# Batch 1's query and even-key sums and batch 2's query sums on GpSimd, noise terms behind the last copy of an expert, zero stores at earlier steps

## The chip, the cores and the metric

The kernel runs on one core of one Trainium2 chip. Its time is the device time of one execution in microseconds (us); lower is better. Engines are named as in the profile: PE is TensorE (PEld its weight loads), DVE is VectorE, ACT is ScalarE, POOL is GpSimd, SP is SyncE, which here only issues transfers.

## The reference

Three stages in a row on 2304 tokens of width 512 (4 batches of 576, 8 heads of 64):

```
q_d, k_d, v_d = means of 4 consecutive positions of q, k, v        # 144 of 576
out_up    = repeat(softmax(scale * q_d k_d^T) v_d, 4)              # pooled attention
out_local = softmax(scale * q k^T  where |i - j| < 4) v            # window attention
x = out_up + out_local                                             # tokens x 512

# first mixture of experts: 8 experts, top 1, only tokens with x @ w_skip > 0
x[do_compute] += gate * relu(x w1[e]) w2[e]

# second: 8 experts, top 2 of  x w_gate + log1p(exp(x w_noise)) * noise
out = sum over the two experts of  weight * relu(x u1[e]) u2[e]
```

## The kernel before

**Attention.** The tokens are cut into 18 tiles of 128. Work on them is a hand-written pipeline of units: `Local(t)` is the window attention of tile t, `Pooled(b, u)` one of five units (u = 4, 0, 1, 2, 3) of the pooled attention of batch b. `push` puts one unit into the pipeline (a slot): its scores on PE, the maximum and subtraction (`soft`) on DVE, then whatever is due in this slot, the exponential on ACT, and the products with the values of the unit three slots earlier, whose results DVE reads out of one of two PSUM banks of the name pB. `schedule(n, f)` puts f into the slot n places on. The instructions of PE, ACT, DVE and POOL stand in just this order in each engine's queue; the order on SP is set by a planner. The slots that matter here: tiles 0 to 2 are slots 0 to 2, tile 3 is slot 3, units (0,4), (0,0), (0,1) are slots 4 to 6, tile 4 is slot 7, (0,2) and (0,3) are 8 and 9, tile 5 is 10, (1,4), (1,0), (1,1) are 11 to 13, tile 6 is 14, (1,2) and (1,3) are 15 and 16.

`load_qk(b)` loads queries into `qT` (two buffers, 128 x 4 x 576) and keys into `kTs[b % 2]` (128 x 2 x 4 x 576: plane 0 for even, plane 1 for odd heads; SP's queue brings plane 0, ACT's plane 1). `pool_qk(b, n)` sums groups of four positions for `Pooled`: n = 0 to 7 are single `tensor_reduce` calls on DVE (line 769), queries into `qd[b]` for even n, even keys into `kd` plane 0 for odd n; four of them go into one slot, four into the next. n = 8 to 10 are odd keys: three whole additions on POOL (line 772), each over 128 x 576 with a stride of four elements on its input. In batch 0 the odd keys are summed on DVE too (line 765).

`load_wall` loads the gate weights before tile 3; three slots later DVE copies them into `wall` (line 1166), which `x_part` of tile 0 first reads in slot 17. `x_add` (line 989) adds the pooled result to a tile on POOL.

**First mixture.** Experts run one after another: `half_up` multiplies with w1 (line 558), `turn` transposes the next expert's tokens (line 537), `down(0)` and `down(1)` multiply with w2 (line 571) and each is followed by a DVE copy of its PSUM bank into `yT` (line 573). `part` of the next expert's loop multiplies `yT` by `wall` (line 579) and so waits for both copies. Into the loop are sprinkled: `clear(i)`, a store of 768 rows of zeros to `out` issued on ACT's queue (line 1668); four of them clear `out` for the second mixture's additions. At expert e = 4 (`E - LATE`): after f2 = 2, `ahead.noisy.load()` reads the logits `l2_d` back (tile `nal`), and at d2 = 0, right behind the first copy, `soft()` puts Exp and Ln of them on ACT and `choose()` the noisy scores and the choice of the second mixture's first experts on DVE (lines 1289 to 1376).

**Second mixture.** Three multiplications of each pair of halves (lines 1576 and 1593); PE works nearly without a pause.

Of the kernel before, what the change touches and what calls it, by code (L numbers as in the profile page):

```python
# [10 lines left out]
F32 = mybir.dt.float32  # L11
# [4 lines left out]
OP = mybir.AluOpType  # L16
# [37 lines left out]
TURN, PART, LOGIT = 1, 2, 3  # L54
PTAG, LTAG, LTAG0 = "pT", "pB", "pW"
LATE = 4
AHEAD = 2
SOFT = 4
LOADW = 41
# [18 lines left out]
NEP = 3  # L78
EPS = 48
ONDVE = (0,)  # L80
NVG = 1
XB = 8
UB = 4
# [18 lines left out]
def moe_attention_kernel(ctx, tc, q, k, v, w_skip, w_gate, w1, w2, g2, n2, noise, u1, u2, out, dbg=None):  # L102
# [507 lines left out]
    with ExitStack() as actx:  # L610
# [135 lines left out]
        def load_qk(b):  # L746

            held["k", b % 2] = b
            qT[b] = at.tile([128, 4, S], F32, name="qT", bufs=2)
            (nc.gpsimd if b == 1 else nc.sync).dma_start(qT[b], q[b])  # L750
            for g in range(2):
                (nc.sync, nc.scalar)[g].dma_start(kTs[b % 2][g:128:2, g], k[b, 64 * g:64 * g + 64])

        def pool_qk(b, n):


            assert held["k", b % 2] == b
            held["kd", b % 2] = (b, n)
            if n == 0:
                qd[b] = at.tile([128, 4, NPOOL], F32, name="qd", bufs=2)  # L760
            kd, kT = kds[b % 2], kTs[b % 2]
            if n >= 8 and b in ONDVE:
                for i in range(n - 8, 4, 3):
                    o, x = kd[:, i, 1], kT[:, 1, i]
                    nc.vector.tensor_reduce(o, x.rearrange("p (g r) -> p g r", r=4), axis=AX.X, op=OP.add)
            elif n < 8:
                i = n // 2
                o, x = (qd[b][:, i], qT[b][:, i]) if n % 2 == 0 else (kd[:, i, 0], kT[:, 0, i])
                nc.vector.tensor_reduce(o, x.rearrange("p (g r) -> p g r", r=4), axis=AX.X, op=OP.add)
            else:  # L770
                o, x = kd[:, :, 1], kT[:, 1].rearrange("p a (g r) -> p a g r", r=4)
                nc.gpsimd.tensor_tensor(o, x[:, :, :, 0] if n == 8 else o, x[:, :, :, n - 7], op=OP.add)
# [255 lines left out]
        def schedule(n, f, *args):  # L1028
            later.setdefault(len(pipe) + n, []).append(lambda: f(*args))
# [132 lines left out]
        def load_wall():  # L1162
            t = at.tile([128, 25, KD], F32, name="gates", bufs=1)
            for o, w in ((0, w_gate), (8, w_skip), (9, g2), (17, n2)):
                nc.gpsimd.dma_start(t[:, o:o + w.shape[1] // KD, :], w.rearrange("p (e k) -> p e k", k=KD))
            schedule(3, lambda: nc.vector.tensor_copy(wall[:, :, 0:25], t.rearrange("p e k -> p k e")))

        pooled_after = {}
        for b in range(B):
# [2 lines left out]
        for t in range(NT):  # L1172
            for b in range(B):
                if LOADQK[b] == t:
                    load_qk(b)
                if POOLQK[b] == t:
                    for n in range(8):
                        schedule(n // QKS, pool_qk, b, n)
                    for n in range(3):
                        schedule(n // 2 if b in ONDVE else n, pool_qk, b, n + 8)  # L1180
                if b == 0 and t == EXP4 and UPE:
                    schedule(0, expansion)
                if POOLV[b] == t:
                    schedule(0, pool_v, b, 0)
                    schedule(VS, pool_v, b, 1)
            if t == 3:
                load_wall()
            if t < 3:
                schedule(0, lambda: None)
                schedule(0, lambda: None)  # L1190
                schedule(0, (start_1, start_2, start_3)[t])
            push(Local(t))
            for b, u in pooled_after.get(t, []):
                push(Pooled(b, u))
# [408 lines left out]
    with ExitStack() as mctx:  # L1603
# [70 lines left out]
        for e in range(E):  # L1674
            x = ex1[e]
            x.wa, x.wb = w1_tiles[e], w2_tiles[e]
            side = []
            if e == E - 2:
                la, side = split_weights(1, 0)
                la()  # L1680
            elif e == E - 1:
                lb, side = split_weights(2, 0)
                lb()
            for f2 in range(KF // 2):
                x.half_up(2 * f2)
                if f2 == 0 and prev is not None:
                    prev.part()
                elif f2 == 3 and e == 0:
                    ahead1.part()
                x.half_up(2 * f2 + 1)  # L1690
                if dbg is not None and "b1" in dbg and f2 == 3:
                    return
                if prev is not None and f2 < len(prev.blocks):
                    prev.finish(f2)()
                if f2 == 2 and e + 3 < E:
                    ex1[e + 3].gather()
                if f2 == 2 and 1 <= e <= 4:
                    clear(6 * (e - 1))
                if e == 0 and f2 == 1:
                    rg1 = m1.tile([128, NT, 3, C1], BF, name="rg1", bufs=1)  # L1700
                    spread(rg1, ohc1, g31, NT, 3, C1)
                if e == 0 and f2 == 2:
                    p = bank("pT", [BLK1, 3, C1])
                    table(p, lhs1, rg1, NT)
                    joined(egt1, p)
                    run(by_rank(gt1, egt1, NB1, rt, "ranked"))
                if e == 0 and f2 == 3:
                    ahead1.finish(0)()
                if e == E - LATE and f2 == 2:
                    ahead.noisy.load()  # L1710
                if e == E - LATE + 1:
                    if f2 == 1:
                        ahead.pl.count()
                        run(ahead.place(0))
                    elif f2 == 2:
                        run(ahead.place(1))
                if e > E - LATE + 1:
                    run(steps, NS)
                if e == E - 1:
                    if f2 < EARLY:  # L1720
                        ex2[0].prep(f2)
                if side and f2 > 1:
                    side.pop(0)()
            if e + 1 < E:
                for b in range(len(ex1[e + 1].blocks)):
                    ex1[e + 1].turn(b)
                load_experts(e + 2, nc.scalar)
            for d2 in range(KD // 2):
                x.down(d2)
                run(side, 1)  # L1730
                if e == E - LATE + 1 and d2 == 0:
                    ahead.tokens()
                    ex2[0].gather(EARLY, ahead.gidx)
                    ex2[1].gather(5 - EARLY, ahead.gidx[:, EARLY:])
                    steps = ahead.gates()
                    run(steps, 6)
                if e == E - LATE and d2 == 0:
                    ahead.noisy.soft()
                    run(ahead.choose())
            prev = x  # L1740
# [211 lines left out]
```

## Time and profile before

| what | us |
|---|---|
| median of 3 runs | 788.83 (785.14 to 790.14) |
| the profiled execution | 785.06 |
| its span, first to last instruction | 783.2 |
| attention, until the first expert's products | about 0 to 136 |
| first mixture | about 136 to 317 |
| second mixture | about 317 to 783 |

| engine | busy us of the span | share |
|---|---|---|
| PE | 755.0 | 96% |
| DVE | 360.1 | 46% |
| ACT | 249.2 | 32% |
| POOL | 239.2 | 31% |

The page's shares are means over stages with different limits, so the argument goes by stretches: the table of windows shows who is busy where, the timelines of PE, DVE, ACT and POOL show what each did in order and what ended its idle time (in brackets: the idle time, and what released it), and the list of issues shows how long transfers took to land.

### The profile page before, as it was taken

The page shows a single profiled execution, that of the slowest core. Times are in us where ns is not written, and L with a number is a line of the kernel's source. Part 1 is how long each engine was busy: PE and PEld are TensorE (multiplying, and loading weights), DVE is VectorE, ACT ScalarE, POOL GpSimd, SP SyncE. Part 2 cuts the span into 40 slices and gives each one's busy share as a digit, 9 for nine tenths or more (in the row PEclk, how much of TensorE's full clock was granted, in tenths as well). Part 3 has the DMA queues.
Part 4 walks back from the last instruction along what each step waited for, and adds up shares of the span by engine and source line. Part 5 has one row for each costly group of instructions (what it writes and reads, how often), then busy time and mean ns, then how long its engine had stood idle before and what let it go on. Part 6 is the DMA issues. An engine that isn't in the chain of part 4 may idle for free.

```text
span 783.2 us, 15164 instructions
## 1 busy us (share of the span) xinstructions
PE 755.0 (96%) x6215; PEld 663.5 (85%) x6215; DVE 360.1 (46%) x817; ACT 249.2 (32%) x492; POOL 239.2 (31%) x248
## 2 busy tenths in 40 slices
PE   6989998999999999999999999999999999999996
PEld 3566785999999899989998898898998997997984
DVE  6997887610111665468864343353242343342200
ACT  3444553111111234224333433243233333333211
POOL 8432422211232341133374305205215115002012
PEclk9899999999999999999999999999999999999999
DMA  8888578699689883331555726426526336333013
GB/s 284 285 250 284 156 191 267 179 369 359 231 281 323 308 311 125 102 69 18 142 188 154 202 81 164 104 81 172 118 84 176 84 110 155 81 87 71 8 16 46
DMA packets 61128, 131.51 MB, mean 168 GB/s; under 512 B 15585, under 2 KB 16928, under 8 KB 59520
## 3 DMA queue, kind: packets, MB, share of 16 engines
q1 hardware_dynamic: 31552, 56.64, 23.0%
q10 hardware_dynamic: 17248, 46.66, 16.5%
q0 software_dynamic: 12256, 27.21, 16.4%
q8 instruction: 50, 0.82, 0.4%
q14 instruction: 22, 0.18, 0.1%
HBM read 101.86 MB, written 23.91 MB: 161 GB/s over the span
## 4 chain that ended last, share of the span: by engine, by line
PE 74%; DMA 2%; issue 2%; DVE 1%; ACT 1%; POOL 0%; POOLq 0%; DVEq 0%; ACTq 0%
PE pY L1593 27%; PE pH L1576 26%; PE pH L558 8%; PE pY L571 8%; PE pT L1561 2%; DMA nal<-l_d 1%; PE pT L590 1%; DMA rows<-x_d,ix2g 1%; PE pT L344 1%; PE pT L537 1%; PE pH L579 0%; POOL out L315 0%; DVE w L335 0%; DMA l_d<-x,ix1w 0%; PE pH L595 0%
## 5 line engine op out<-in xcount | busy, mean ns | idle before, releaser
L1593 PE MATMUL pY<-w,hh 128*128 128x512 f32 (+6 forms) x640 | 201.5, 396 | 0.0
L1576 PE MATMUL pH<-xh,w 128*128 128x256 f32 (+7 forms) x1024 | 195.9, 303 | 0.0
L1576 PEld LDWEIGHTS pH<-xh,w 128*128 128x128 f32 x1024 | 162.9, 188 | 0.8
L1593 PEld LDWEIGHTS pY<-w,hh 128*128 128x128 f32 (+6 forms) x640 | 115.0, 183 | 27.4
L1252 DVE TENSOR_TENSOR w<-stg,w 128x1024 fp32r<-128x1024 f32 x64 | 82.6, 1297 | 108.5 <-ACT w L1251 108.4
L1593 PE MATMUL pY<-w,hl 128*128 128x512 f32 (+6 forms) x320 | 125.6, 392 | 0.0
L1576 PE MATMUL pH<-xl,w 128*128 128x256 f32 (+7 forms) x512 | 123.5, 302 | 0.0
L1581 DVE SCALAR_TENSOR_TENSOR hl<-pH,hh 128x256 fp32r<-128x256 f32 (+7 forms) x128 | 57.0, 474 | 128.5 <-ACT hh L1580 128.4
L315 POOL DMA_INDIRECT out<-yo,ix2w x35 | 68.8, 1967 | 130.0 <-ACT yo L1595 121.5
L1580 ACT ACTIVATE hh<-pH 128x256 fp32r<-128x256 f32 (+7 forms) x128 | 49.2, 424 | 151.9 <-PE pH L1576 151.7
L1576 PEld LDWEIGHTS pH<-xl,w 128*128 128x128 f32 x512 | 90.2, 188 | 0.0
L310 POOL DMA_INDIRECT rows<-x_d,ix2g x32 | 36.2, 1131 | 155.6 <-PE pT L1561 144.7
L1593 PEld LDWEIGHTS pY<-w,hl 128*128 128x128 f32 (+6 forms) x320 | 58.5, 183 | 15.5
L571 PE MATMUL pY<-hT,w 128*128 128x112 f32 (+7 forms) x512 | 69.2, 296 | 0.0
L1251 ACT ACTIVATE w<-stg 128x1024 fp32r<-128x1024 f32 x64 | 66.9, 1054 | 7.4 <-DMA stg<-in_moe_w 7.4
L1595 ACT ACTIVATE yo<-pY,gt 128x512 f32<-128x512 f32 (+6 forms) x35 | 24.1, 687 | 138.1 <-PE pY L1593 77.2
L571 PEld LDWEIGHTS pY<-hT,w 128*128 128x128 f32 x512 | 67.4, 190 | 0.2
L558 PE MATMUL pH<-xT,w 128*128 128x200 f32 (+6 forms) x448 | 66.2, 301 | 0.0
L558 PEld LDWEIGHTS pH<-xT,w 128*128 128x128 f32 x448 | 61.1, 190 | 1.8 <-issue 1.7
L315 POOL DMA_INDIRECT l_d<-x,ix1w x15 | 14.3, 956 | 91.9 <-DVE x L598 91.0
L573 DVE COPY yT<-pY 128x224 f32<-128x224 f32 (+7 forms) x16 | 7.5, 471 | 70.0 <-PE pY L571 70.0
L989 POOL TENSOR_TENSOR x<-x,up 128x512 f32<-128x512 f32 x15 | 19.1, 1276 | 44.0 <-DMA up<-od 35.8
(422 smaller groups left out, 844.2 us busy)
## 6 DMA issues: line engine op xcount, KB each, us to landing
w<-in_moe_w ACTq DMA_DIRECT2D x16, 2048.0 KB, 12.6
stg<-in_moe_w SPq DMA_DIRECT2D x64, 512.0 KB, 3.5
x_d<-x SPq DMA_DIRECT2D x18, 264.0 KB, 4.6
out<-zero ACTq DMA_DIRECT2D x3, 1536.0 KB, 7.6
up<-od SPq DMA_DIRECT2D x14, 256.0 KB, 5.9
qT<-in_q SPq DMA_DIRECT2D x3, 1152.0 KB, 5.5
vw<-in_v SPq DMA_DIRECT2D x18, 192.0 KB, 5.4
vw<-in_v ACTq DMA_DIRECT2D x18, 192.0 KB, 5.1
```

Of the source, the lines that this page charges most:

```text
L310: return nc.gpsimd.indirect_dma_start(out=dst, out_offset=None, in_=x_d[0:n + 1], in_offset=bass.IndirectOffsetOnAxis(ap=idx, axis=0))
L315: return nc.gpsimd.indirect_dma_start(out=dst, out_offset=bass.IndirectOffsetOnAxis(ap=idx, axis=0), in_=src, in_offset=None, **kw)
L558: nc.tensor.matmul(self.p[:, j], w[:, k, f * 128:(f + 1) * 128], self.xT[:, k], start=k == 0, stop=k == KD - 1)
L571: nc.tensor.matmul(p[:, j], w[:, f, d * 128:(d + 1) * 128], self.hT[:, f], start=f == 0, stop=f == KF - 1)
L989: e.tensor_tensor(xs[t][:, 0:DM], xs[t][:, 0:DM], ups[t], op=OP.add)
L1251: nc.scalar.activation(hi[:, c], st[i], AF.Copy)
L1252: V.tensor_tensor(lo[:, c], st[i], hi[:, c].bitcast(F32), op=OP.subtract)
L1576: nc.tensor.matmul(p, w[:, k, fs], self.x[ch][n][:, k, 0:ch[1] - ch[0]], start=k == 0 and i == 0, stop=k == KD - 1 and i == 2)
L1580: nc.scalar.activation(hi, p, AF.Relu)
L1581: V.scalar_tensor_tensor(lo, p, 0.0, hi.bitcast(F32), op0=OP.max, op1=OP.subtract)
L1593: nc.tensor.matmul(p, h[:, f], w[:, f], start=f == 0 and i == 0, stop=f == KF - 1 and i == 2)
L1595: nc.scalar.activation(o, p, AF.Copy, scale=gate[0:n])
```

## The change

Sums of batch 1's queries and even keys move from DVE to POOL: three whole additions each, in front of the odd keys' three in slot 7. Batch 2's query sums move to POOL in slot 10, the slot in which its queries are loaded; its even keys stay on DVE. The copy into `wall` goes from the third slot after the load to the twelfth (slot 15). In the first mixture the zero stores are issued at (e, f2) = (1,2), (2,0), (2,2), (3,1) in place of (1,2), (2,2), (3,2), (4,2), and `soft` and `choose` follow `down(1)` of expert 4 in place of `down(0)`.

```diff
+CLEARS = ((1, 2), (2, 0), (2, 2), (3, 1))
+ONPOOLQ, ONPOOLQD, QDP, WALLP = (1,), (2,), 0, 12
...
+        def pooled_on_gpsimd(o, x):
+            x = x.rearrange("p a (g r) -> p a g r", r=4)
+            for j in range(1, 4):
+                nc.gpsimd.tensor_tensor(o, x[:, :, :, 0] if j == 1 else o, x[:, :, :, j], op=OP.add)
+
+        def pool_q(b):
+            qd[b] = at.tile([128, 4, NPOOL], F32, name="qd", bufs=2)
+            pooled_on_gpsimd(qd[b], qT[b])
+
         def pool_qk(b, n):
...
-            if n == 0:
+            if n == 0 and b not in ONPOOLQD:
                 qd[b] = at.tile([128, 4, NPOOL], F32, name="qd", bufs=2)
...
+            elif b in ONPOOLQ and n < 8:
+                if n == 0:
+                    pooled_on_gpsimd(kd[:, :, 0], kT[:, 0])
+                    pooled_on_gpsimd(qd[b], qT[b])
+            elif n % 2 == 0 and n < 8 and b in ONPOOLQD:
+                pass
             elif n < 8:
...
-            schedule(3, lambda: nc.vector.tensor_copy(wall[:, :, 0:25], t.rearrange("p e k -> p k e")))
+            schedule(WALLP, lambda: nc.vector.tensor_copy(wall[:, :, 0:25], t.rearrange("p e k -> p k e")))
...
                     load_qk(b)
+                    if b in ONPOOLQD:
+                        schedule(QDP, pool_q, b)
...
-                if f2 == 2 and 1 <= e <= 4:
-                    clear(6 * (e - 1))
+                if (e, f2) in CLEARS:
+                    clear(6 * CLEARS.index((e, f2)))
...
-                if e == E - LATE and d2 == 0:
+                if e == E - LATE and d2 == KD // 2 - 1:
                     ahead.noisy.soft()
                     run(ahead.choose())
```

## Rows read from the trace of the kernel before

**Rows 1.** Busy us of each engine in each stretch, granted clock, DMA share, GB/s
```profile
27.00:62.00 35.00, 31.54 (x511) 21.93 (x508) 32.91 (x76) 14.09 (x32) 13.16 (x9) 0.98 0.81 246
62.00:125.00 63.00, 61.17 (x1131) 47.27 (x1127) 50.59 (x147) 33.69 (x90) 19.77 (x15) 1.00 0.72 207
...
152.00:300.00 148.00, 144.92 (x1190) 139.34 (x1190) 39.69 (x103) 27.76 (x62) 41.52 (x41) 1.00 0.85 301
```

**Rows 2.** Timeline of PE: start, us, what [idle before, its releaser]
```profile
40.44 0.85 PE L849 MATMUL pB<-vd,epT 128*128 128x130 f32 x6 [0.58 <-DVE or L860]
...
44.36 1.08 PE L978 MATMUL pB<-vw,eT 128*32 128x128 f32 x32 [1.66 <-issue]
45.33 0.69 PE L815 MATMUL pA<-kd,qd 128*32 128x288 f32 x8
...
60.99 1.08 PE L978 MATMUL pB<-vw,eT 128*32 128x128 f32 x32 [1.22 <-issue]
```

**Rows 3.** Timeline of DVE, attention
```profile
1.55 1.98 DVE L134 MEMSET kT<- 128x2304 f32 x1 [0.43 <-issue]
...
33.55 1.31 DVE L1166 COPY wall<-gates 128x100 f32<-128x100 f32 x1
...
41.14 0.74 DVE L769 TENSOR_REDUCE qd<-qT 128x144 f32<-128x576 f32 x1
...
43.12 0.74 DVE L769 TENSOR_REDUCE kd<-kT 128x144 f32<-128x576 f32 x1
...
43.97 0.29 DVE L860 TENSOR_TENSOR od<-pB,rp 128x128 f32<-128x128 f32 x1
...
59.74 0.74 DVE L769 TENSOR_REDUCE kd<-kT 128x144 f32<-128x576 f32 x1
...
60.59 0.29 DVE L860 TENSOR_TENSOR od<-pB,rp 128x128 f32<-128x128 f32 x1
```

**Rows 4.** Timeline of POOL, attention
```profile
0.72 2.02 POOL L135 MEMSET kT<- 128x2304 f32 x1 [0.29 <-POOLq L1941]
...
18.23 0.63 POOL L750 DMA_DIRECT2D qT<-in_q  x1
...
23.92 0.53 POOL L1165 DMA_DIRECT2D gates<-in_moe_w_noise  x1
29.90 1.25 POOL L772 TENSOR_TENSOR kd<-kT 128x576 f32<-128x576 f32 x1 [5.45 <-DMA kT<-in_k]
31.23 3.52 POOL L772 TENSOR_TENSOR kd<-kd,kT 128x576 f32<-128x576 f32 x2
```

**Rows 5.** Transfers issued from 9 to 19 us: KB each, us to landing
```profile
qT<-in_q POOLq DMA_DIRECT2D x1, 1152.0 KB, 9.8
...
kT<-in_k SPq DMA_DIRECT2D x1, 576.0 KB, 10.7
```

**Rows 6.** Timeline of SP: the issue of batch 1's even keys
```profile
11.48 0.51 SPq L752 DMA_DIRECT2D kT<-in_k  x1
```

**Rows 7.** DVE's subtraction of the pooled units: duration ns min/median/max, first and last start
```profile
L824 DVE TENSOR_TENSOR ep<-pA,mxp x20: 457/458/458, 28.3 to 106.6; 128x288 f32<-128x288 f32 x20
```

**Rows 8.** Timeline of PE, expert 5's first step
```profile
260.20 0.45 PE L579 MATMUL pH<-yT,wall 128*32 128x152 f32 x4 [1.77 <-DVE yT L573]
```

**Rows 9.** Timeline of DVE, the choice, the copy behind it, and what follows
```profile
257.30 0.31 DVE L1289 TENSOR_TENSOR nasp<-nasp,nz 128x144 f32<-128x144 f32 x1 [3.85 <-ACT nasp L1286]
...
259.68 0.47 DVE L573 COPY yT<-pY 128x304 f32<-128x304 f32 x1
262.42 0.23 DVE L598 SCALAR_TENSOR_TENSOR x<-pH,gt,xr 112x16 f32<-112x16 f32 x1 [2.27 <-PE pH L595]
```

**Rows 10.** Timeline of ACT: the last zero store
```profile
245.84 0.40 ACTq L1668 DMA_DIRECT2D out<-zero  x1
```

**Rows 11.** Chain of waits from 243 to 260 us, in order of time
```profile
246.60 8.69 DMA nal<-l_d
```

**Rows 12.** DMA issues of the page: KB each, us to landing
```profile
w<-l_d SPq DMA_DIRECT2D x1, 144.0 KB, 3.1
```

## The prediction

> **What bounds the kernel now.** I read the page first, then the windows, then the timelines of the two places that the change touches. The windows [rows 1] say where a gain can come from. From 27 to 62 us, where batches 0 to 2 are pooled, PE is busy 31.54 of 35 us and DVE 32.91: two engines in order, both close to full, so each wait of PE there is worth a look. From 62 to 125 us PE is busy 61.17 of 63, from 152 to 300 it is 144.92 of 148. So PE sets the end in nearly every stretch, and what the change can give is PE's idle time, not DVE's busy time: 3.46 us from 27 to 62, 3.08 from 152 to 300. A gain made early is kept if what follows is started by the work before it and not by a transfer of its own pace; I come back to that below.
>
> PE's idle time in the first stretch is three pieces [rows 2]: 0.58 us before 40.44 (released by DVE's line 860), 1.66 before 44.36 and 1.22 before 60.99. Together they are 3.46, all of it. The two put down to "issue" have a cause that DVE's timeline shows [rows 3]: the products at 44.36 and 60.99 write a pB bank, and DVE's reading of one ends at 43.97 + 0.29 = 44.26 and 60.59 + 0.29 = 60.88, each about 0.1 us before PE starts. Both readings stand right behind a block of four sums on line 769: the last of a block starts at 43.12 and at 59.74. So the sums of batch 1 (two blocks) cost PE 0.58 + 1.66, and those of batch 2 cost it 1.22.
>
> In the first mixture the wait is 1.77 us before 260.20 [rows 8]: `part` of expert 5 waits for the second copy into `yT`, which DVE does at 259.68 behind `choose`, which begins at 257.30, released by ACT [rows 9]. ACT had waited for `nal`, whose transfer took 8.69 us from 246.60 [rows 11].
>
> **The sums of batch 1.** Away from DVE: eight sums. In a block the first starts at 41.14, the fourth at 43.12, a pitch of 0.66 us [rows 3], so 8 x 0.66 = 5.3 us leave DVE, 2.64 before each of the two readings that PE waited for. The waits of 0.58 and 1.66 are both shorter than that, so both go whole: 2.24 us. The cover for it is POOL, and POOL must be done before PE wants `kd` and `qd[1]`, which was at 45.33 [rows 2] and becomes 45.33 - 2.24 = 43.09.
>
> What three additions cost is in the trace, with the same shape, stride and engine: 29.90 to 31.23 + 3.52 = 34.75, so 4.85 us with the gaps [rows 4]. POOL now has three such triples for batch 1 (even keys, queries, odd keys): 14.55 us. When the first may begin is the one open point. POOL is free at 23.92 + 0.53 = 24.45 [rows 4]. The even keys are plane 0, issued on SP at 11.48 [rows 6] and landed 10.7 us later [rows 5], at 22.2. The queries were issued at 18.23 [rows 4] and land 9.8 later [rows 5], at 28.0. The wait until 29.90 is for the odd plane. If waits go by plane, the even keys run 24.45 to 29.3, the queries to 34.15, the odd keys to 39.0: 4 us before PE's 43.09, and the whole 2.24 is gained. If a wait goes by the whole tile, nothing starts before 29.90 and the chain ends at 29.90 + 14.55 = 44.45; with 0.1 us for the release PE starts at 44.55 and the gain is 45.33 - 44.55 = 0.8. I take the first: the two planes of the other key tile were filled by DVE from 1.55 to 3.53 [rows 3] and by POOL from 0.72 to 2.74 [rows 4], side by side, so order is kept by plane.
>
> **The query sums of batch 2.** Four sums (2.64 us) leave DVE, two in each of slots 14 and 15; the four even keys stay. The wait of 1.22 before 60.99 sits behind the second block. On POOL the triple comes behind batch 1's (39.0, or 44.45), so it ends by 49.3 at the latest; its odd keys follow, 4.85 more, 54.2, and batch 2's first unit wants them only some slots after 60.99. Nobody waits.
>
> **The copy into `wall`.** At 33.55 it took 1.31 us for 100 elements, and ended at 34.86, 0.1 after POOL's additions at 34.75 [rows 3, 4]: it stood still until POOL was done. Out of slot 6 this frees DVE of 1.31; PE had no wait there, so it is worth nothing by itself. In slot 15 POOL is at work again. The copy costs from about 0.3 us (if POOL pauses) to about 1.9 (one addition of 1.76 to the end, and 0.1). DVE has lost 2.64 before the reading at 60.59, so the net relief there is 2.64 - 1.9 = 0.7 to 2.64 - 0.3 = 2.3 against a wait of 1.22: gain 0.7 to 1.22, I take 1.05, nearer the upper end since POOL has pauses. If POOL blocked DVE's other work as well, the case would turn; the subtraction of the pooled units took 457 to 458 ns in all 20 [rows 7], the ones under POOL's additions from 29.90 to 34.75 among them, so it does not.
>
> The Trainium skill, "SBUF — State Buffer", section "Who interferes with whom", has a rule that speaks against this change: VectorE and GpSimd share a pair of ports, the second to come is blocked for the whole instruction, and copies and VectorE instructions with both inputs in SBUF are the ones that take it, while reductions do not. The trace agrees for the copy (1.31 us) and for the subtraction with one input in PSUM (458 ns); by the rule the sums here come out the same.
>
> **The noise terms and the zero stores.** With `choose` behind the second copy, that copy runs when its bank is ready, and PE goes on at 260.20 - 1.77 = 258.43. `choose` took 257.30 to 259.68 on DVE [rows 9]; with a copy of 0.47 in front of it, it ends at 260.15 at the latest. Queued behind it is line 598, which takes expert 4's rows out of PSUM for their scatter; it came at 262.42, released by PE [rows 9], and is wanted 1.77 earlier, at 260.65: 0.5 us of room. ACT has the Ln done before 257.30, and its next work is `part`'s result, which PE can't give before 258.43. So the 1.77 goes whole; if either queue were late, what PE would wait for next is line 598's bank.
>
> Four zero stores stay four, with the same bytes. The last leaves 245.84 [rows 10], 0.8 us ahead of `nal`, which took 8.69 us, where a load of the same size took 3.1 [rows 12]. That makes `nal` up to 5.6 us earlier; it buys room for the same 1.77, not more. Where they go, PE is near full and DMA at 0.85, 301 GB/s [rows 1]: hidden by PE's work on weights that were loaded before. If that cover were gone, one store of 768 rows x 512 x 4 bytes = 1.57 MB would cost 5.2 us at that rate.
>
> **The sum.** 2.24 + 1.05 + 1.77 = 5.06, say 5.1 us. Against the profiled execution that is 785.06 - 5.1 = 780.0. The median of the runs shown is 3.8 above that execution, so for the median I forecast 788.83 - 5.1 = 783.7. The ends: nothing of the three terms or all (3.46 + 1.77 = 5.2).
>
> **Rivals.**
> *POOL is late.* The wait goes by the whole tile: 0.8 + 1.05 + 1.77 = 3.6, 785.2. For it: POOL did stand until 29.90. Against: the two planes filled side by side.
> *The early gain is given back.* From 62 on DMA could set the pace: 0.72 from 62 to 125, with batch 3's loads among it. Then only the 1.77 stays: 787.1. Against: these loads are issued when PE frees their buffers, so they move with it.
> *Slower: POOL becomes the bound.* Place: PE's first unit of batch 1. It decides from the point where POOL's chain ends later than 45.33, thus with a triple above (45.33 - 29.90) / 3 = 5.1 us when it starts at 29.90, or 7.0 when at 24.45. At 1.5 times the row's price and the late start the chain ends at 29.90 + 21.8 = 51.7, PE loses 6.4 us, and with 1.05 and 1.77 gained the time is 3.6 above: 792.4. Against: the price is that of the same instruction, measured under DVE's sums.
> *The stall in the first mixture stays,* because ACT or the rows' copies come late behind `choose`: 3.3 gained, 785.5.
> *More than the sum,* by waits that hide in PE's pipelined rows: over 8 us, below 781.
>
> **Chances.** The forecast 0.45, POOL late 0.17, given back 0.14, the stall stays 0.08, slower 0.06, more than the sum 0.10. Runs of this kernel lie 5 us apart (785.14 to 790.14), so a difference of 1% (7.9 us) is about what a measurement can tell. All but the last two cases lie within it: same 0.84; faster 0.12, nearly all of it the last case, with the forecast's upper end and a fast median; slower 0.04, the part of that case with a still higher price. The range: its upper end takes in the gain given back (787.1) with 0.9 of scatter, its lower end the whole 5.2 with a median that falls to the fast execution (779.9): 779.5 to 788.0. Outside are "slower" and most of "more".
>
> **What would show it.** Right: PE's idle time from 27 to 62 falls from 3.46 to under 0.6; POOL starts batch 1's even keys before 29.90 and ends the odd ones near 39; the copy into `wall` near 54 us takes 0.3 to 1.9; no wait before `part` of expert 5, and `nal` lands in less than 8.69. Wrong: a wait of PE at batch 1's first unit with POOL as releaser; the first expert's products no earlier than before although the early waits are gone; a new wait of PE for rows or weights between 194 and 260. My forecast is wrong if the price of POOL's additions differs under other neighbours, or if SP's planner orders the loads otherwise.

## The result, and the profile after

The changed kernel takes 779.71 us in the median of 16 runs (775.73 to 783.81), the kernel before 786.77 (16 runs, 782.12 to 790.14): a ratio of 0.9914 with an interval of 0.9893 to 0.9935, so 6.8 us less, 5.1 to 8.4. The forecast was 783.7 with a gain of 5.1: the side, a change within 1% and the range (779.5 to 788.0) were right, but the time lies only 0.2 inside the range's lower end, and the forecast gain is the lowest that the interval allows. The profiled execution of after took 780.45 us (span 778.5; before 785.06, span 783.2). That is 4.6 less and close to the 780.0 of the sum, but, as will be seen, not by the sum's terms.

The line numbers of after are up to 21 higher: L759 and L789 are GpSimd's sums, L786 VectorE's, L829 and L832 the pooled scores, L877 the read-out of pB, L995 the value products, L1183 the copy into `wall`, L575 the copy into `yT`, L581 `part`, L600 the taking out of the rows.

The windows (us, then busy time and instructions of PE, PE's weight load, DVE, ACT and POOL, granted clock, DMA share, GB/s), beside [rows 1]:

```profile
27.00:62.00 35.00, 32.97 (x549) 24.07 (x542) 26.50 (x65) 15.21 (x34) 27.13 (x18) 0.95 0.89 254
152.00:300.00 148.00, 147.37 (x1217) 141.83 (x1216) 41.97 (x106) 28.79 (x63) 45.09 (x44) 1.00 0.87 305
```

The sums moved as meant: from 27 to 62 DVE is busy 6.4 us less and POOL 14.0 more. PE's idle time there fell only from 3.46 to 2.03, and the granted clock of this stretch is 0.95 where it was 0.98. From 152 to 300 the idle time fell from 3.08 to 0.63. That is the stall of 1.77 and a wait of 0.68, which has only slipped to the other side of the window's edge (145 to 152 has it now).

Where PE's idle time is, by its timeline, with the half-speed rows behind it:

```profile
42.97 0.69 PE L832 MATMUL pA<-kd,qd 128*32 128x288 f32 x8 [1.85 <-POOL kd L789]
43.59 0.55 PE L852 MATMUL pT<-ident,ep 128*128 128x128 f32 x3
43.97 1.27 PE L866 MATMUL pB<-vd,epT 128*128 128x130 f32 x6
45.04 1.27 PE L829 MATMUL pA<-kd,qd 128*128 128x288 f32 x2
...
54.84 0.70 PE L829 MATMUL pA<-kd,qd 128*128 128x288 f32 x2
...
58.24 1.08 PE L995 MATMUL pB<-vw,eT 128*32 128x128 f32 x32
...
65.31 0.69 PE L832 MATMUL pA<-kd,qd 128*32 128x288 f32 x8
```

The three waits of [rows 2] are gone: nothing in brackets before the read-outs or at 58.24. In their place stands one new wait of 1.85 us, on GpSimd's odd keys, and behind it the products take 1.27 where the same ones take 0.78 and 0.70 at full speed. The windows of single microseconds show the clock at half (the lower of its two levels, 1.2 of 2.4 GHz); the same stretch of before is at 1.00 throughout, though it had a wait of 1.66 in front of it:

```profile
44.00:45.00 1.00, 1.00 (x8) 1.00 (x7) 0.64 (x2) 0.77 (x2) 0.92 (x2) 0.54 1.08 440
45.00:46.00 1.00, 1.00 (x4) 0.71 (x4) 0.46 (x2) 0.15 (x1) 0.92 (x2) 0.50 0.96 388
46.00:47.00 1.00, 1.00 (x6) 0.90 (x5) 0.55 (x2) 0.00 (x0) 1.00 (x1) 0.50 0.99 276
47.00:48.00 1.00, 1.00 (x8) 1.00 (x8) 0.37 (x1) 0.80 (x2) 0.67 (x1) 0.75 0.62 124
```

POOL's timeline, beside [rows 4]:

```profile
23.91 0.53 POOL L1182 DMA_DIRECT2D gates<-in_moe_w_noise  x1
28.38 1.29 POOL L759 TENSOR_TENSOR kd<-kT 128x576 f32<-128x576 f32 x1 [3.94 <-DMA kT<-in_k]
29.74 3.51 POOL L759 TENSOR_TENSOR kd<-kd,kT 128x576 f32<-128x576 f32 x2
33.20 1.34 POOL L759 TENSOR_TENSOR qd<-qT 128x576 f32<-128x576 f32 x1
...
39.42 3.49 POOL L789 TENSOR_TENSOR kd<-kd,kT 128x576 f32<-128x576 f32 x2
42.87 1.25 POOL L759 TENSOR_TENSOR qd<-qT 128x576 f32<-128x576 f32 x1
```

The price of a triple was right: 28.38 to 42.91 is 14.53 for three, forecast 14.55. The start was not: 28.38 where 24.45 was taken. The issues show why (KB each, us to landing):

```profile
kT<-in_k SPq DMA_DIRECT2D x1, 576.0 KB, 10.9
kT<-in_k ACTq DMA_DIRECT2D x1, 576.0 KB, 9.4
```

SP's half (even keys) was issued at 11.14 and landed at 22.0, ScalarE's half (odd keys) was issued at 18.82 and landed at 28.2. The first addition touches the even keys alone, and it started 0.2 us after the odd ones had landed.

The copy into `wall`, and the first mixture, by DVE's timeline (beside [rows 3, 9]):

```profile
55.04 0.67 DVE L1183 COPY wall<-gates 128x100 f32<-128x100 f32 x1
...
254.96 0.47 DVE L575 COPY yT<-pY 128x304 f32<-128x304 f32 x1 [3.66 <-PE pY L573]
255.35 0.30 DVE L1308 TENSOR_TENSOR nasp<-nasp,nz 128x144 f32<-128x144 f32 x1
...
257.62 0.18 DVE L1395 SCALAR_TENSOR_TENSOR nasel<-nacnt,early 128x18 bf16<-128x18 f32 x1
258.06 0.23 DVE L600 SCALAR_TENSOR_TENSOR x<-pH,gt,xr 112x16 f32<-112x16 f32 x1 [0.25 <-PE pH L597]
```

The second copy now runs when PE's product is ready, `choose` ends at 257.80, and line 600 still waits for PE and not for `choose`. `part` has no wait. How much that is worth, PE's timelines show by their starts, first before, then after:

```profile
257.99 0.45 PE L579 MATMUL pH<-yT,wall 128*32 128x152 f32 x4
...
260.59 1.25 PE L558 MATMUL pH<-xT,w 128*128 128x144 f32 x8
```

```profile
255.83 0.47 PE L581 MATMUL pH<-yT,wall 128*32 128x152 f32 x8
256.22 1.25 PE L560 MATMUL pH<-xT,w 128*128 128x144 f32 x8
```

From the start of `part` to the products behind it before takes 2.60 us and after 0.39: 2.21 less, where the bracket of [rows 8] says 1.77. The rest is the group itself: cut in two it takes 0.45 twice (at 257.99 and, in [rows 8], at 260.20), whole it takes 0.47. No bracket shows that part.

`nal` was issued at 243.98 and ScalarE went on at 248.53, 4.55 later, where [rows 11] have 8.69.

From about 470 us to the end after stays 4.54 us ahead of before. Over all 14 profiles shown here and below, the stretch from VectorE's first copy into `yT` (165 us in after) to its ninth (251) takes 85.6 to 86.0, and that from its last (310) to the end 468.6 to 469.4. So nearly all that differs between executions lies in front of the first copy or between the ninth and the last.

### The profile page after: what moved, and what is told of

Read it like the earlier page. It is cut to its first block, busy times and chain, and to the rows that moved or that the text cites. A ratio compares the mean times of both kernels' runs of the same rounds, so it can differ in the third digit from the quotient of the medians.

```text
span 778.5 us, 15158 instructions
## 1 busy us (share of the span) xinstructions
PE 755.6 (97%) x6215; PEld 664.3 (85%) x6215; DVE 351.3 (45%) x805; ACT 249.6 (32%) x492; POOL 255.0 (33%) x257
## 4 chain that ended last, share of the span: by engine, by line
PE 76%; issue 2%; DVE 1%; DMA 1%; POOL 0%; ACT 0%; POOLq 0%; DVEq 0%; ACTq 0%
PE pY L1612 27%; PE pH L1595 26%; PE pH L560 9%; PE pY L573 9%; PE pT L1580 2%; PE pT L592 1%; PE pT L539 1%; DMA rows<-x_d,ix2g 1%; PE pT L346 1%; PE pH L581 0%; POOL out L317 0%; DVE w L337 0%; PE pH L597 0%; PE pT L223 0%; DVE hl L1600 0%
## 5 line engine op out<-in xcount | busy, mean ns | idle before, releaser
L575 DVE COPY yT<-pY 128x224 f32<-128x224 f32 (+7 forms) x16 | 7.5, 471 | 73.8 <-PE pY L573 73.8
```

## The experiments

All kernels are after with the edit shown; medians and ratios are against before on the same chip (medians of 784.95 to 786.17 there). The runs also list a mean granted clock: 0.989 for before (63 executions), 0.990 for after (16).

**The two halves of the change.** The first kernel, attn_only, has the sums and the copy, with the first mixture as before; moe_only is the reverse.

```
--- attn_only
-                if (e, f2) in CLEARS:
-                    clear(6 * CLEARS.index((e, f2)))
+                if f2 == 2 and 1 <= e <= 4:
+                    clear(6 * (e - 1))
-                if e == E - LATE and d2 == KD // 2 - 1:
+                if e == E - LATE and d2 == 0:
--- moe_only
-ONPOOLQ, ONPOOLQD, QDP, WALLP = (1,), (2,), 0, 12
+ONPOOLQ, ONPOOLQD, QDP, WALLP = (), (), 0, 3
```

> The attention part of the change alone: sums on GpSimd and the copy into wall in slot 15; zero stores and noise terms as before. Theory (the two parts add, and each is worth the PE waits that it takes away): in the changed kernel's profile batch 1's first unit started 2.4 us earlier than before, then lost about 1.6 to a clock at half speed and won 1.3 at the reading of batch 2's products; net of the later start that is 2.5 to 3.5 us of the whole, so 783.5 to 784.5 beside 786.8 before, with the 1.77 us wait of TensorE before part of expert 5 still there. Rival (the early gain is lost later, and the first mixture carries the result): within 1 us of before. Second rival (the attention part is worth the rest of the median's 7 us): 5 us faster.

> The first mixture's part alone: noise terms behind the last copy and zero stores sooner; all sums on VectorE as before. Theory: the 1.77 us wait goes whole and nothing else changes: 1.8 us faster than before (785.0 beside 786.8), TensorE idle from 152 to 300 us falls from 3.08 to about 1.3. Rival (zero stores at earlier steps also speed up what stands behind the old places, gathers and weights): 3.5 us or more. Rival (they cost as much as is gained): no difference.

attn_only: 784.21 (12 runs), 0.9968 [0.9949, 0.9987], 2.5 us less. moe_only: 783.36 (9 runs), 0.9960 [0.9945, 0.9976], 3.1 us less. Together 5.6 of the 6.8. In attn_only's profile GpSimd starts batch 1 at 24.53, as forecast, and PE has no wait from 40 to 60. The stall is still there, and the clock falls behind it (timeline of PE, then windows):

```profile
257.26 0.45 PE L581 MATMUL pH<-yT,wall 128*32 128x152 f32 x4 [1.94 <-DVE yT L575]
```

```profile
255.00:260.00 5.00, 3.06 (x23) 2.51 (x21) 1.96 (x9) 0.71 (x2) 0.00 (x0) 0.87 1.02 411
260.00:265.00 5.00, 5.00 (x48) 4.72 (x49) 2.04 (x6) 0.41 (x1) 2.58 (x3) 0.79 1.04 385
```

Its lead over before, 2.94 us at that copy into `yT`, is 1.28 at the next: some 1.7 us were lost beyond the wait. moe_only's profile has the same elsewhere: a wait of 1.57 for the first expert's rows, and behind it a group of products that takes 3.83 in after and 6.07 here:

```profile
133.89 1.01 PE L539 MATMUL pT<-ident,xr 112*128 112x112 f32 x4 [1.57 <-DMA xr<-x_d,ix0g]
...
135.53 6.07 PE L560 MATMUL pH<-wide,w 128*128 128x112 f32 x32 [0.17 <-ACT wide L540]
```

So a wait of PE can cost more than its length. How often, the next runs ask.

moe_only's expectation, that only the wait of 1.77 goes and PE's idle time from 152 to 300 falls to about 1.3, was missed in its profile: the idle time is 2.72, since PE stands twice more behind `part`, for 0.44 and 0.86, put down to "issue". That goes with the chip and not with an edit. From VectorE's ninth copy into `yT` to its last, the six profiles without the stall that were taken on chips 6 and 0 (moe_only, even_on_dve, warm_fill, choose_only, clears_only, b1_only) need 59.9 to 61.2 us; after and the four of chip 3 need 59.1, before 61.3. The cause is open, so the stall's worth is read from before and after alone.

**GpSimd's lateness and the clock.** even_on_dve puts batch 1's even keys back on VectorE (GpSimd keeps the queries and the odd keys); warm_fill puts five useless products before the value products near 43 us.

```
--- even_on_dve
-ONPOOLQ, ONPOOLQD, QDP, WALLP = (1,), (2,), 0, 12
+ONPOOLQ, ONPOOLQD, QDP, WALLP = (), (1, 2), 0, 12
+                    if b == 1 and b in ONPOOLQD:
+                        schedule(0, pool_q, b)
--- warm_fill
-FILLS = {2: 2}
+FILLS = {2: 2, 11: 5}
```

> The changed kernel, but batch 1's even keys are summed on VectorE again; its queries stay on GpSimd, before the odd keys. Theory (GpSimd's chain of three triples began only at 28.38, with the landing of the odd plane's transfer, ended at 42.91, made TensorE wait 1.85 us, and the wait dropped its clock to half for 3.5 us): two triples of 4.85 us from about 28.4 end near 38.1, the wait of TensorE at batch 1's first unit is gone, the clock stays at 1.0, and of the 3.4 us so freed VectorE's four sums (1.3 us in each of two slots) take back 0.5 at most: 2 to 3 us faster than the changed kernel. Rival (the clock fall cost nothing that stays, the next units wait anyway): 0.5 us or less. Rival (VectorE's sums bring back the old waits of 0.58 and 1.66): no faster.

> The changed kernel with five products of 128 x 512 of no use (about 0.2 us each) on TensorE in slot 10, right before the wait for GpSimd; they leave nothing out and add nothing to the result. Theory (the wait of 1.85 us drops the clock): they fill 1 us of the wait, the granted clock stays at 1.0 from 43 to 48 us, and the kernel is up to 1.6 us faster than the changed one. Rival (the clock falls for another reason): the same wait's end at about 43.0, the clock at 0.5 from 44 to 47, no difference.

even_on_dve: 779.61 (6 runs), 0.9924 [0.9903, 0.9945]. warm_fill: 779.19 (6 runs), 0.9913 [0.9895, 0.9932]. Neither differs from after's 0.9914; the theories, 2 to 3 and up to 1.6 us faster, were both missed. even_on_dve's profile has no wait of PE from 40 to 50 and the clock at 1.00:

```profile
40.00:50.00 10.00, 10.00 (x177) 6.92 (x173) 9.31 (x25) 5.49 (x12) 6.83 (x5) 1.00 0.91 255
```

If after's wait of 1.85 with the half clock behind it, 3.7 us, came in every execution, even_on_dve would be that much faster, a ratio near 0.987, which its interval excludes. So the profiled execution of after does not stand for all of them. In warm_fill's profile GpSimd started at 24.54, near the forecast.

**The two edits of the first mixture.** choose_only has the choice behind the last copy but the stores as before; clears_only has the stores sooner but the choice in front. Both have the sums as before.

```
--- choose_only (beside moe_only's edit)
-                if (e, f2) in CLEARS:
-                    clear(6 * CLEARS.index((e, f2)))
+                if f2 == 2 and 1 <= e <= 4:
+                    clear(6 * (e - 1))
--- clears_only (beside moe_only's edit)
-                if e == E - LATE and d2 == KD // 2 - 1:
+                if e == E - LATE and d2 == 0:
```

> The kernel before with one edit: the noise terms' choice behind the second copy into yT; zero stores and sums as before. Theory (the order on VectorE is what PE waited for): the wait of 1.77 us before part of expert 5 is gone although nal still takes about 8.7 us; choose then ends at 257.9 + 0.47 + 2.4 = 260.8 or so and line 598's successor at most 0.2 later than wanted: 1.6 to 1.8 us faster, ratio about 0.998 at the same granted clock. Rival (the late load is the cause, and the order only moves the wait): choose ends near 260.8 whatever is in front of it, PE next waits for line 600's bank or ACT, and the ratio stays within 0.999 to 1.001.

> The kernel before with one edit: the zero stores sooner; the choice stays in front of the second copy. Theory (nal's 8.69 us are queueing behind the last zero store): nal lands 4 to 5 us after its issue as in the changed kernel (4.55), choose starts 2.0 us later near 253.5 and is over before PE has the second copy's bank near 257.9; the wait of 1.77 is gone by this edit alone, ratio about 0.998. Rival (the order is the cause): nal is earlier but PE still waits 0.5 us or more there; gain under 1 us, ratio over 0.9987. If both edits alone give 1.77, the two in the change overlap and one would have done.

choose_only: 783.55 (12 runs), 0.9963 [0.9942, 0.9985]. clears_only: 782.80 (7 runs), 0.9946 [0.9919, 0.9973]. Each removes the stall alone. choose_only, by ACT's and DVE's timelines (`nal` was issued at 244.55):

```profile
253.20 0.32 ACT L1304 ACTIVATE nasp<-nal 128x144 f32<-128x144 f32 x1 [4.67 <-DMA nal<-l_d]
```

```profile
255.04 0.47 DVE L575 COPY yT<-pY 128x304 f32<-128x304 f32 x1 [3.66 <-PE pY L573]
...
258.14 0.23 DVE L600 SCALAR_TENSOR_TENSOR x<-pH,gt,xr 112x16 f32<-112x16 f32 x1 [0.25 <-PE pH L597]
```

`nal` still takes 8.65 us and ScalarE waits for it, but PE does not any more. clears_only, by DVE's timeline (`nal` issued at 246.55, ScalarE goes on at 251.16):

```profile
253.15 0.31 DVE L1308 TENSOR_TENSOR nasp<-nasp,nz 128x144 f32<-128x144 f32 x1 [0.38 <-ACT nasp L1305]
...
255.43 0.18 DVE L1395 SCALAR_TENSOR_TENSOR nasel<-nacnt,early 128x18 bf16<-128x18 f32 x1
256.42 0.47 DVE L575 COPY yT<-pY 128x304 f32<-128x304 f32 x1 [0.81 <-PE pY L573]
```

The choice is over 0.8 us before the copy's bank is ready. In neither profile does `part` of expert 5 wait.

**Filling the stall instead of removing it.** stall_filled is attn_only with seven useless products in `part`'s wait.

```
             for k in range(KD):
+                if k == KD // 2 and self.cap == CAPS[E - LATE]:
+                    wq = bank("pT", [128, 512])
+                    for i in range(7):
+                        nc.tensor.matmul(wq, warm[:, 0:128], warm, start=True, stop=True)
```

> The sums on GpSimd as in the changed kernel, choice and zero stores as before, and seven useless 128x512 bf16 products (about 1.5 us) put into the wait of part of expert 5. The wait is not shortened, only filled; the useful work is that of the run with the sums alone (784.21, ratio 0.9968, where the clock fell behind this wait and about 1.7 us were lost). Theory (a wait of PE costs its length and, in some executions, a fall of the granted clock behind it): the clock stays at 1.00 from 255 to 270, the mean granted clock of the executions rises by 0.001 or more over 0.9887, and the time falls by 0.5 to 1.5 us, ratio 0.995 to 0.9965. Rival (the falls have nothing to do with the wait): mean clock and ratio as in that run, 0.9887 and 0.9968, or worse by what the products delay.

782.22 (8 runs), 0.9934 [0.9908, 0.9960]; mean clock 0.9904 where attn_only had 0.9887. In the profile the products take 1.69 of the wait, 0.21 is left, and the clock stays at 1.00 from 255 to 270 (0.87 and 0.79 in attn_only). The median is 2.0 below attn_only's, but on another chip, and the two intervals overlap. Its profile is that of its slowest run (789.76). The direction is the theory's; neither the effect nor its size is shown.

**The batches one by one.** b1_only keeps batch 1's sums on GpSimd and puts batch 2's queries back on VectorE; b2_only the reverse. Both have the new first mixture.

```
--- b1_only
-ONPOOLQ, ONPOOLQD, QDP, WALLP = (1,), (2,), 0, 12
+ONPOOLQ, ONPOOLQD, QDP, WALLP = (1,), (), 0, 12
--- b2_only
-ONPOOLQ, ONPOOLQD, QDP, WALLP = (1,), (2,), 0, 12
+ONPOOLQ, ONPOOLQD, QDP, WALLP = (), (2,), 0, 12
```

> The changed kernel, but batch 2's query sums back on VectorE (slots 14 and 15); batch 1's queries and even keys stay on GpSimd. Theory: the wait of about 1.2 before the value products near 61 us comes back and takes 1.05 to 1.2 us of the gain: ratio 0.9927 to 0.993 where the changed kernel has 0.9914. Rival (batch 2's products are held by something else, or the wait is made up later): no wait there or the same time as the changed kernel, 0.9914.

> The changed kernel, but batch 1's sums back on VectorE; batch 2's query sums stay on GpSimd, and so does the wall copy in slot 15. Theory (the two batches' terms are coupled: TensorE's wait near 61 us is 1.2 behind batch 1's waits and was 1.98 in the kernel with batch 1's sums moved alone): from batch 1's last pooled score of its first pair to batch 2's first the stretch is 12.0 us before and 10.4 to 11.2 here, no wait before the value products near 60 us; together with the 1.8 of the first mixture 3.0 to 3.6 faster than before, ratio 0.9955 to 0.996. Rival (the terms are independent, and the undersized part is batch 1's): the same stretch, but batch 1's removal alone must then show 3.9 at the same clock, and this kernel is about 2.8 faster, ratio 0.9964.

b1_only: 781.91 (8 runs), 0.9942 [0.9917, 0.9968]. b2_only: 781.38 (12 runs), 0.9945 [0.9921, 0.9969]. PE's timeline of b1_only, with the last pooled score of batch 1 and the first of batch 2 around the wait:

```profile
53.73 0.70 PE L829 MATMUL pA<-kd,qd 128*128 128x288 f32 x2
59.18 1.08 PE L995 MATMUL pB<-vw,eT 128*32 128x128 f32 x32 [1.98 <-issue]
66.21 0.69 PE L832 MATMUL pA<-kd,qd 128*32 128x288 f32 x8
```

and the same of b2_only:

```profile
54.73 0.70 PE L829 MATMUL pA<-kd,qd 128*128 128x288 f32 x2
58.44 1.08 PE L995 MATMUL pB<-vw,eT 128*32 128x128 f32 x32 [0.24 <-issue]
65.64 0.69 PE L832 MATMUL pA<-kd,qd 128*32 128x288 f32 x8
```

With batch 1's waits gone, PE comes to batch 2's block earlier and waits 1.98 there, not the 1.22 of [rows 2]. The two terms are coupled.

**The rest.** warm_more has useless products in more of PE's waits, wall_3 the copy into `wall` back in slot 6, both_on_sp both halves of batch 1's keys on SP's queue.

```
--- warm_more
-FILLS = {2: 2}
-BUSY = {"turn15": 1, "table": 2, "turn16": 3, "part16": 1, "end": 3}
+FILLS = {2: 2, 11: 5}
+BUSY = {"turn15": 3, "table": 2, "logits15": 3, "turn16": 3, "part16": 2, "end": 6}
--- wall_3
-ONPOOLQ, ONPOOLQD, QDP, WALLP = (1,), (2,), 0, 12
+ONPOOLQ, ONPOOLQD, QDP, WALLP = (1,), (2,), 0, 3
--- both_on_sp
-                (nc.sync, nc.scalar)[g].dma_start(kTs[b % 2][g:128:2, g], k[b, 64 * g:64 * g + 64])
+                (nc.sync, nc.sync if b == 1 else nc.scalar)[g].dma_start(kTs[b % 2][g:128:2, g], k[b, 64 * g:64 * g + 64])
```

> The changed kernel with 13 more useless products where TensorE waits: five around 43 us, and eight between 120 and 133 us, in the waits of the last tiles (0.77 and 0.83) and before the first expert's rows. Theory (falls of the granted clock behind these waits cost time): the mean granted clock rises from 0.990 to 0.993 or more, no stretch of the profile from 40 to 145 us is under 1.00, and the time falls by 0.5 to 1.5 us against the changed kernel: ratio 0.9895 to 0.991. Rival (the fall is made up elsewhere, or the products delay the work as much as the clock gives): clock up, ratio within 0.001 of 0.9914, or above it.

> The changed kernel with the copy into wall back in slot 6. Theory: GpSimd is in batch 1's sums there, the copy takes 0.67 to 1.9 us, but TensorE's waits for VectorE around it are gone with the sums, so it costs at most 0.3: ratio 0.9910 to 0.992, and the reading of pB near 61 us is 0.7 earlier for nothing. Rival (the copy's place was part of the gain): a wait of TensorE of 0.5 us or more between 31 and 44 us, ratio 0.992 to 0.993.

> The changed kernel with both halves of batch 1's keys issued on SP instead of one on ScalarE's queue. Theory (GpSimd's first addition waits for both halves, and in the changed kernel's profile the half on ScalarE's queue came 6.2 us after the other): both land by 25, the even keys start at 24.5 and the chain of the three sums ends by 39.5; where the changed kernel's profile had a wait of 1.85 at 42.97 there is none. Over many executions that wait is rare (even keys on VectorE gave 0.9924 against 0.9914), so the time is the same: 0.9905 to 0.9925. Rival (GpSimd is late in most executions and this is worth its 1.85 and the clock behind it): ratio 0.988 to 0.9895. A third: the half takes SP's queue from batch 0's values, the start is 0.5 us or more later, ratio over 0.993.

warm_more: 779.36 (7 runs), 0.9917 [0.9882, 0.9952]. The mean clock rises to 0.9936, the highest of all kernels, and the time does not fall: the rival was right. The products lie in PE's order and cost their own time wherever the wait is shorter than they are (1.08 us near 43, by the table below). One fall remained, 0.83 from 130 to 140, behind a wait of 1.1 for the first expert's rows.

wall_3: 779.96 (9 runs), 0.9931 [0.9905, 0.9956]. The ratio is in the rival's range, but the interval holds after's, so these runs can't tell whether the copy's place was part of the gain. The copy took 1.05 us at 31.71; the one long wait of PE in the rival's stretch, 1.42 before 42.34, was for GpSimd's odd keys and not for VectorE.

both_on_sp: 778.55 (6 runs), 0.9906 [0.9869, 0.9943]. GpSimd starts at 24.95; it then stood 2.2 us for the queries, and its chain ended at 41.64, where PE's first pooled score starts at 41.70, so PE lost 0.3 at most (A in the table below). It is the lowest median, and its interval holds after's ratio: the same, as the theory had it. Its timeline of POOL, and that of wall_3:

```profile
24.95 1.21 POOL L759 TENSOR_TENSOR kd<-kT 128x576 f32<-128x576 f32 x1 [0.45 <-DMA kT<-in_k]
```

```profile
27.80 1.24 POOL L759 TENSOR_TENSOR kd<-kT 128x576 f32<-128x576 f32 x1 [3.24 <-DMA kT<-in_k]
```

In both_on_sp the even half landed at 22.0 and the other at 24.8; in wall_3 the even half landed at 21.6.

**One table of the profiles.** Us between the starts of pooled-score products in PE's timelines (as those above: in after 37.08, 42.97, 54.84 and 65.31): from batch 0's last to batch 1's first (A), from there to batch 1's last (B), from there to batch 2's first (C).

| kernel | batch 1 sums | batch 2 queries | A | B | C | sum |
|---|---|---|---|---|---|---|
| before | VectorE | VectorE | 6.61 | 10.68 | 12.01 | 29.30 |
| moe_only | VectorE | VectorE | 6.49 | 10.68 | 12.02 | 29.19 |
| choose_only | VectorE | VectorE | 6.94 | 10.98 | 11.71 | 29.63 |
| clears_only | VectorE | VectorE | 5.31 | 10.67 | 12.02 | 28.00 |
| b2_only | VectorE | GpSimd | 5.38 | 10.66 | 10.91 | 26.95 |
| b1_only | GpSimd | VectorE | 3.85 | 10.20 | 12.48 | 26.53 |
| attn_only | GpSimd | GpSimd | 3.86 | 10.20 | 11.19 | 25.25 |
| even_on_dve | GpSimd, even keys VectorE | GpSimd | 3.86 | 10.20 | 10.43 | 24.49 |
| stall_filled | GpSimd | GpSimd | 3.85 | 10.20 | 10.43 | 24.48 |
| both_on_sp | GpSimd | GpSimd | 4.16 | 10.22 | 10.43 | 24.81 |
| wall_3 (PE waits 1.42 for GpSimd) | GpSimd | GpSimd | 5.46 | 10.22 | 10.43 | 26.11 |
| after (waits 1.85, clock at half) | GpSimd | GpSimd | 5.89 | 11.87 | 10.47 | 28.23 |
| warm_fill (five useless products) | GpSimd | GpSimd | 4.94 | 10.20 | 10.87 | 26.01 |
| warm_more (five useless products) | GpSimd | GpSimd | 4.93 | 10.20 | 10.43 | 25.56 |

Undisturbed the sums' part is worth 29.30 - 24.49 = 4.8 us here (3.5 to 5.1 with moe_only, choose_only or clears_only in place of before). With GpSimd late and the clock at half, as in the profile of after, it is worth 29.30 - 28.23 = 1.07.

## Why the prediction was right, and where it was not

**The sums of batch 1, forecast 2.24.** The waits named were the right ones and they go whole. The term was too small: A falls from 6.61 to 3.86 and B from 10.68 to 10.20, together 3.2. (A with the sums on VectorE lies between 5.31 and 6.94 over five profiles, so the term is not one number: 1.9 to 3.6.) The forecast counted the two waits that the rows show in brackets. PE's groups also hold short delays that no bracket shows: A fell by 2.75 for 2.24 of bracketed waits, and the pitch of the first pooled scores of batch 1 went from 1.78 and 1.87 to 1.60 and 1.59. The rival "more than the sum, by waits that hide in PE's pipelined rows" named this, with too little weight.

**"Waits go by plane": the step that failed.** The inference came from two fills of the other tile that ran side by side. A fill has no transfer to wait for, so the pair said nothing of how the first reader of two half-loads waits. In after's profile the addition of the even keys began 0.2 us after the odd keys' half had landed, and 6 us after its own; in both_on_sp 0.15 after the second half and 3 after its own; in wall_3, stall_filled and warm_more too it stood for a transfer of `kT` until 27.80, 26.63 and 25.52, with its own half there since 21.6, 21.3 and 20.6. So the first reader waits for both halves. The sign that the prediction itself named for being wrong, a wait of PE at batch 1's first unit with POOL as releaser, is in after's profile, and the odd keys ended at 42.91 and not near 39. The forecast's start was nevertheless met, or nearly, in four profiles (24.53, 24.54, 24.56 and 24.95). In attn_only, one of them, ScalarE's half was issued at 16.99, in after at 18.82; in both_on_sp it went by SP. Of the eight profiled kernels with the even keys on GpSimd, PE waited for it in two (after 1.85, wall_3 1.42). The rival "POOL is late" is thus true of some executions: by its sum it would have cost 1.4 of the 2.24, and after's profile has 1.85 and the clock.

**The query sums of batch 2, forecast 1.05.** C falls from 12.01 to 10.43, by 1.6. From before alone b2_only gains 1.1, nearly the forecast; behind batch 1's gain, b1_only shows 12.48, and 2.05 is gained. The forecast added two waits as if each stood alone, while the first had hidden part of the second.

**The copy into `wall`, forecast 0.3 to 1.9.** Measured 0.67, and 0.55 to 1.59 in the eight other profiles with it in that slot; with GpSimd idle beside it, in moe_only, choose_only and clears_only, it took 0.24 to 0.26. In after it ended at 55.71 and GpSimd's addition at 55.59; in wall_3 at 32.76 and 32.65; before, [rows 3, 4], at 34.86 and 34.75. Three times it ended 0.11 to 0.12 us behind an addition: it stands still until that one is done, and not until the next. The Trainium skill, "SBUF — State Buffer", section "Who interferes with whom", says that a copy on VectorE and an instruction on GpSimd can block each other, for the whole length of the one that came first. These rows agree.

**The first mixture, forecast 1.77.** The mechanism is shown: order alone and the load alone each remove the wait. The term was too small here too: by PE's starts the wait cost 2.2, not the 1.77 of its bracket. So "the 0.5 us of room" was enough (line 600 is released by PE in after and in choose_only), and that an earlier `nal` "buys room for the same 1.77, not more" was right but incomplete, since it needs no reordering at all. In the medians the three kernels with only such edits gain 3.1, 2.9 and 4.2 us by their ratios, and the lower ends of their intervals are 1.9, 1.2 and 2.1. Part of what is above 1.77 goes with the clock: their mean granted clocks are 0.9894, 0.9914 and 0.9909 beside 0.9889. Fitted over 181 executions with a mean of its own for each kernel (before's from three chips together), time falls by 4.1 us (plus or minus 1) per 0.01 of the mean clock, and at equal clock the three gain 2.5, 1.5 and 3.0 (plus or minus 1.1 to 1.3). That no longer differs from 1.77 or 2.2; the fit shows that time and clock go together, not which causes which.

**The zero stores.** Where they went they cost nothing: PE is busy all of 194 to 252 before and after.

**That the early gain is not given back** is borne out by attn_only's runs (2.5 us less) and only in part by profiles. From batch 2's first pooled score to VectorE's first copy into `yT` before needs 99.3 us and after 99.9, so after lost 0.55 of its 2.71 there; but without stall_filled (107.6, with the clock at half) the profiles lie between 99.0 and 102.4 in this stretch, with the change and without, and can't tell 0.55 from chance.

**The sum.** 4.8 + 2.2 = 7.0 is what the undisturbed profiles give, beside a measured 6.8 (5.1 to 8.4) and a forecast of 5.1; at equal clock the measured gain is 5.6 (plus or minus 0.9). GpSimd's lateness in some executions takes back up to 3.7. So all three terms named the right wait and were too small, by 1.9 together, and against that stood a lateness that was given too little. Of the 4.0 us by which the time was missed, 2.1 come from the base: the forecast started at 788.83, the median of three runs, and sixteen give 786.77. That the time still fell into the range, by 0.2, was luck in part: the lower end allowed for a fast median, not for larger terms. The profile of after alone would have misled: its 4.54 us are 1.64 of an earlier start (batch 0's last pooled score at 37.08 and not 38.72, which lay between 36.23 and 39.68 over the profiles, with and without the change alike), 1.07 in A to C and 2.2 in the first mixture, less the 0.55 between them, and small ones.

**What stays open.** How often GpSimd is late, and what that costs in the median. Why the clock falls behind some waits of PE and not behind others; and whether its fall behind the old stall is why attn_only gained only 2.5 in its runs while its profile has 4.05 in A to C. stall_filled points that way and doesn't settle it. No version was shown to beat after; both_on_sp comes nearest.

## What to carry to other kernels

Two waits of one engine that lie behind each other are one chain: removing the first moves the engine towards the second, so read the second's true size from the slower engine's work, not from its bracket; and where a wait cuts a group of products in two, compare starts, since the bracket leaves a part out (1.77 for 2.21 here). When a load is split over two queues, take the later half as the start of every reader, unless the trace shows a reader that started between the halves. And one profile of the changed kernel is one draw: its gain was near the forecast in size and not in its places, which only the parts' own runs and several profiles side by side could show.

## What the runs showed of the hardware

A wait of PE sometimes costs more than its length. Behind waits of 1.57 (moe_only), 1.85 (after), 1.94 (attn_only) and 1.89 (stall_filled, near 79 us) the granted clock fell to half or towards it for some microseconds, costing some 1.7 us in after (B 11.87 for 10.20) and 2.2 in moe_only (6.07 for 3.83). The same came behind shorter waits for the first expert's rows: 1.11 (warm_more), 1.22 (b1_only) and 1.41 (wall_3). Behind 1.66 and 1.77 in before, 1.42 in wall_3 and 1.98 in b1_only it did not, so the length of the wait alone does not decide it. Useless products in the waits went with a higher mean granted clock (0.9925 and 0.9936 beside 0.990) and won no time that the runs can tell. The start moves the whole kernel: batch 0's last pooled score came between 36.23 and 39.68 us over 14 profiles, a spread larger than any single part of this change is worth. The waits of PE in front of it are for transfers (4.50 for values in after, 3.67 and 3.07 for values and keys in before).
